# Moving the FFN units of a fused attention and mixture-of-depths kernel between scores and values, and the row fetch into a step of its own

## The chip, the cores and the metric

The kernel runs on one core of one Trainium2 chip. The metric is the device time of one execution in microseconds (us), the median of several runs. The core has a matrix engine (TensorE, PE in the profile, with its weight loads as PEld), a vector engine (VectorE, DVE), a scalar engine for activations and copies (ScalarE, ACT), a general engine (GpSimd, POOL) and a queue that issues most of the transfers (SyncE, SP).

## The reference

Attention with queries that are averaged in pairs is followed by a mixture of depths: in each batch the 128 tokens with the highest gate score go through a two-layer FFN, and the others pass unchanged.

```python
# q, k, v: (8, 8, 1152, 64) float32 = B, H, S, D
q_pool = q.reshape(B, H, S // 2, 2, D).mean(axis=3)
scores = scale * np.matmul(q_pool, k.transpose(0, 1, 3, 2))   # 576 x 1152 per head
attn = softmax(scores)                                        # over the 1152 keys
x = np.matmul(attn, v)            # then (B, S, H*D): 8 x 576 tokens x 512

scores = np.einsum('bsd,d->bs', x, w_gate)
out = x.copy()
for b in range(B):
    top_idx = np.argpartition(-scores[b], 128)[:128]
    xe = x[b, top_idx]
    ye = np.maximum(xe @ w1, 0.0) @ w2         # w1: 512 x 1024, w2: 1024 x 512
    g = 1.0 / (1.0 + np.exp(-scores[b, top_idx]))
    out[b, top_idx] = x[b, top_idx] + g[:, None] * ye
```

## The kernel before

Two heads of one batch are a pair; there are 32 pairs. The 576 pooled queries of a pair are worked in two halves of 288, so there are 64 halves, 8 to a batch. One turn `h` of the main loop issues the scores of half `h` and the values of half `h - 1`. The order in which instructions are issued here is the order in which each engine's queue gets them; nothing reorders them.

```python
for h in range(n_halves + 1):
    if h < n_halves:
        ...                                  # loads two pairs ahead; store of x
        self.scores(half)                    # PE L818, ACT exponentials L825
        if h > 1:
            of = halves[h - 2 - s]["pair"]
            if s == 0:                       # even half
                of["groups"] = self.side_by_side(of["sum"]...)   # ACT L887
            else:                            # odd half
                self.spread(of)              # ACT L902: total -> sums
        if h > 2:
            self.gated(halves[h - 3])        # DVE red, part; starts a batch's routing
        self.folded(half)                    # POOL acc L857, DVE fold L862, sum L872
        if h > 1:
            self.multiplied(halves[h - 2])   # POOL prod L925
        if s == 0 and loaded:
            upcoming = loaded
            self.prepare_pair(upcoming)      # POOL qp, DVE kT, qT of the next pair
    ...
    if h > 0:
        done = halves[h - 1]
        self.weighted(done)                  # PE L836, ACT two L844, POOL av L846
        self.drained(done)                   # DVE avb
    ...
    if 1 < h < n_halves and s == 0:
        done["pair"]["total"] = self.added(done["pair"]["groups"])   # DVE L893
    ...
    elif h > 2 and s == 1:
        self.normalized(halves[h - 2]["pair"])    # DVE rec, POOL x
    if h < n_halves:
        self.units()                         # one step of every batch's routing
```

The scores of a half are nine tiles of 128 keys, each in one PSUM tile of two banks. There are four such tiles, used in turn for everything that TensorE writes (`self.psum = pool("psum", 4, space=psum)`). An exponential on ScalarE takes each score tile to `p`, of which there are two buffers. The row sums of `p` come from `folded`: GpSimd adds the first two thirds of `p` into `acc`, and VectorE sums the last third and then `acc`.

The routing of a batch is a Python generator; each `yield` ends a step, and a call of `units()` runs one step of every batch in flight, the newest batch first. It starts in `gated` when a batch's last pair is done. Cut to what the engines do, for every batch but the last:

```python
def routed(self, b, part):
    nc.vector.tensor_reduce(line, part ...)           # the batch's gate scores
    yield True
    if b < self.B - 2:
        groups = self.side_by_side(line)              # ACT L887, 4 copies
        yield True
        total = self.added(groups)                    # DVE
    else:
        ...                                           # batch 6: one matmul, one copy
    ... sync DMAs: total -> row in DRAM -> sc_row, sc # scores on all partitions
    yield True
    if b < self.B - 2:
        yield True
    nc.gpsimd.tensor_scalar(gate ...)                 # POOL
    for t, rows in tiles:                             # rank of each token: comparisons
        ... 3 DVE operations per tile of tokens
        if t in (1, 3):
            yield True
    nc.scalar.activation(gate, gate, AF.Exp, scale=-1.0) ...
    ... sync DMAs: both -> row_rank in DRAM -> lines  # ranks and gates, all partitions
    yield True
    for of, to in ((self.token_line, found), (lines[:, :, 1, :], own_gate)):
        nc.vector.scalar_tensor_tensor(pick, lines, self.token, of ...)  # search, DVE
    nc.gpsimd.tensor_scalar(index, found ...)         # POOL
    nc.gpsimd.indirect_dma_start(xe <- rows_out[index])   # fetch of the rows
    yield True
    yield True
    ... 4 transposes of xe on PE (L1192); nc.scalar.copy(xeT)
    yield True
    ... first layer: 2 x 16 matmuls (L1203); ACT hT = relu, twice (L1211)
    yield "hidden" ...
    ... second layer: 8 matmuls (L1216)
    nc.scalar.activation(y, ps, AF.Copy, scale=own_gate)  # ACT L1235
    nc.gpsimd.tensor_tensor(xe = y + xe)              # POOL L1238
    nc.gpsimd.indirect_dma_start(rows_out[index] <- xe)   # rows written back
    yield True
```

The matmul steps inside the layers yield `False`, which does not end a step. Batch 5 stops after its first layer (`"hidden"`) and its second layer is kept for the end of the kernel, where batches 6 and 7 finish. Scores are written to the output by `stored` before the rows are fetched from there.

Of the kernel before, what the change touches and what calls it, by code (L numbers as in the profile page):

```python
# [21 lines left out]
def _rows_of(ap_1d: bass.AP, parts: int) -> bass.AP:  # L22

    return dataclasses.replace(ap_1d, ap=[[0, parts]] + [list(x) for x in ap_1d.ap])
# [3 lines left out]
def _any_scores(  # L28
# [446 lines left out]
    def run(units):  # L475
        for _ in units:
            pass
# [50 lines left out]
    for _ in range(2):  # L528
        advance(None)
        one, two = None, one  # L530
    run(routing)
    run(routed(B - 1, x))


class _Plain:
# [461 lines left out]
    def routed(self, b, part):  # L997
# [12 lines left out]
        if b < self.B - 1:  # L1010

            yield True
            if b < self.B - 2:
                groups = self.side_by_side(line)
                yield True
                total = self.added(groups)
            else:
                total = self.small.tile([BLK, self.QB], F32, name="total")
                ps = self.banks()[:, 0, 0 : self.QB]
                nc.tensor.matmul(  # L1020
                    ps,
                    lhsT=self.merge.rearrange("p g j -> p (g j)"),
                    rhs=line[:, :],
                    start=True,
                    stop=True,
                )
                nc.scalar.copy(total[:, :], ps[0:BLK, :])
            sc_row = ffn.tile([P, NT * P], F32, name="sc_row")
            row = self.dram.tile([Sp], F32, name="row")
            nc.gpsimd.memset(sc[:, NF:], 0.0)  # L1030
            nc.sync.dma_start(row.rearrange("(i n) -> i n", i=BLK), total[:, :])
            nc.sync.dma_start(sc_row[:, 0:Sp], _rows_of(row[:], P))
            nc.sync.dma_start(sc[:, 0:NF], row[0 : NF * P].rearrange("(t p) -> p t", p=P))
            nc.sync.dma_start(
                sc[0 : self.TAIL, NF:], row[NF * P :].rearrange("(t p) -> p t", p=self.TAIL)
# [6 lines that stand above are left out]
            diag = ffn.tile([P, self.QB, BLK], F32, name="diag", bufs=1)  # L1042
            nc.vector.tensor_tensor(
                out=diag[:, :, :],
                in0=line[:, :].unsqueeze(2).broadcast_to([P, self.QB, BLK]),
                in1=self.same[:, :].unsqueeze(1).broadcast_to([P, self.QB, BLK]),
                op=ALU.mult,
            )
            yield True
            sc_row = self.line_of_scores()  # L1050
            ps = self.banks()
            for s in range(2):
                nc.tensor.matmul(  # L1053
                    ps[:, s, 0 : self.HALF],
                    lhsT=self.ones[:, :],
                    rhs=diag[:, s * self.HB : (s + 1) * self.HB, :].rearrange("p n i -> p (n i)"),
                    start=True,
                    stop=True,
                )
            nc.scalar.copy(  # L1060
                sc_row[:, 0:Sp].rearrange("p (i s n) -> p s n i", s=2, n=self.HB),
                ps[:, :, 0 : self.HALF].rearrange("p s (n i) -> p s n i", i=BLK),
            )
            yield True
            self.columns(sc, sc_row)
# [66 lines left out]
        for s0, w in self.slots:  # L1132
# [3 lines left out]
            if b == self.B - 1:  # L1136

                nc.vector.tensor_tensor(
                    out=pick[:, :, 0:w],
                    in0=self.slot_f[:, s0 : s0 + w].unsqueeze(1).broadcast_to([P, NT, w]),  # L1140
                    in1=rank[:, :].unsqueeze(2).broadcast_to([P, NT, w]),
                    op=ALU.is_equal,
                )
                yield True
                ps = self.banks()[:, 0, 0:2]
                for t, rows in tiles:
                    nc.tensor.matmul(  # L1147
                        ps[0:w, :],
                        lhsT=pick[0:rows, t, 0:w],
                        rhs=meta[0:rows, t, :],  # L1150
                        start=(t == 0),
                        stop=(t == NT - 1),
                    )
                nc.scalar.copy(index[0:w, :], ps[0:w, 0:1])
                nc.scalar.copy(own_gate[0:w, :], ps[0:w, 1:2])
            else:
                yield True

                found = self.small.tile([P, 1], F32, name="found_token")
                for of, to in ((self.token_line, found), (lines[:, :, 1, :], own_gate)):  # L1160
                    nc.vector.scalar_tensor_tensor(
                        out=pick.rearrange("p t i -> p (t i)").rearrange("p (i t) -> p i t", t=NT)[0:w],
                        in0=lines[0:w, :, 0, :],
                        scalar=self.token[0:w, s0 // P : s0 // P + 1],
                        in1=of[0:w, :, :],
                        op0=ALU.is_equal,
                        op1=ALU.mult,
                        accum_out=to[0:w, :],
                    )
                nc.gpsimd.tensor_scalar(  # L1170
                    out=index[0:w, :],
                    in0=found[0:w, :],
                    scalar1=float(b * Sp),
                    scalar2=None,
                    op0=ALU.add,
                )
# [106 lines left out]
        )  # L1283
        return count_i

    def units(self):

        for entry in self.routing[::-1]:
            b, unit = entry
            if b in self.waiting:  # L1290
                continue
            end = next((mark for mark in unit if mark), None)
            if end is None:
                self.routing.remove(entry)
            elif end == "hidden" and b == self.B - 3:
                self.waiting.add(b)

    def run(self):
# [14 lines left out]
        for h in range(n_halves + 1):  # L1313
            if h < n_halves:
                n, s = divmod(h, 2)
                if s == 0:
                    pair = upcoming
                    if pair["hp"] == 0:
                        part = self.ffn.tile([P, self.NPAIR, self.QB], F32, name="part")
                    pair["part"] = part  # L1320
                else:
                    loaded = None
                    if n + 2 < len(pairs):
                        loaded = self.load_pair(*pairs[n + 2])
                        self.load_values(loaded)
                    if n > 1:
                        self.stored(halves[h - 4]["pair"])
                if h > 1:
                    next(weights, None)
                half = {"pair": pair, "s": s}  # L1330
                halves.append(half)
                self.scores(half)
                if h > 1:

                    of = halves[h - 2 - s]["pair"]
                    if s == 0:
                        of["groups"] = self.side_by_side(of["sum"].rearrange("p j n -> p (j n)"))
                    else:
                        self.spread(of)
                if h > 2:  # L1340
                    self.gated(halves[h - 3])
                self.folded(half)
                if h > 1:
                    self.multiplied(halves[h - 2])
                if s == 0 and loaded:
                    upcoming = loaded
                    self.prepare_pair(upcoming)
            else:
                self.stored(halves[h - 3]["pair"])
                self.gated(halves[h - 3])  # L1350
                self.multiplied(halves[h - 2])
                self.units()
            if h > 0:
                done = halves[h - 1]
                self.weighted(done)
                self.drained(done)
            if h == n_halves:
                self.multiplied(done)
                self.gated(halves[h - 2])
            if 1 < h < n_halves and s == 0:  # L1360
                done["pair"]["total"] = self.added(done["pair"]["groups"])
            if h == n_halves:
                self.normalized(done["pair"])
            elif h > 2 and s == 1:
                self.normalized(halves[h - 2]["pair"])
            if h < n_halves:
                self.units()
        for _ in weights:
            pass

# [90 lines left out]
```

## Time and profile before

| what | value |
|---|---|
| time, median of 3 runs | 708.12 us (708.08 to 708.34) |
| span of the profiled execution | 706.3 us |
| mean granted TensorE clock | 0.999 |
| transfers | 82.86 MB, mean 117 GB/s |
| scores matmuls L818 | 4608 records, 296.0 us busy |
| values matmuls L836 | 4608 records, 294.1 us busy |
| first FFN layer L1203 | 512 records, 59.3 us busy |
| second FFN layer L1216 | 128 records, 57.3 us busy |
| exponentials L825 | 576, mean 691 ns, 319.2 us busy |
| acc L857 on GpSimd | 192, mean 1413 ns, 266.1 us busy |

How to read it: a float32 matmul leaves two records, so 36 matmuls of a half are 72 records in a chain or a timeline. Busy times of matmuls count the time between start and end of pipelined instructions, so waiting that is shorter than the pipeline is not seen as idle. Line numbers are those of the kernel before; in the changed kernel the lines after the first edit lie one to six further on. In a timeline the columns are the start in us, the length in us, the engine, the line, the operation, output and input with their shapes, the count, and in brackets the idle time of the engine ahead of it with what ended that. In the chain of waits the columns are start, length, engine and what.

### The profile page before, as it was taken

To read this page: it belongs to the slowest core of one execution; us is meant where nothing else is said; L and a number is where in the kernel's file an instruction comes from. 1 tells how busy PE (TensorE), PEld (TensorE's weight loads), DVE (VectorE), ACT (ScalarE), POOL (GpSimd) and SP (SyncE) were. 2 spreads that over 40 slices of the span, in tenths; PEclk is the share of its full clock that TensorE was granted. 3 is DMA by queue.
4 is the path that set the end of the run, shared out by engine and by line. 5 is a ranking of instruction groups with operands and counts; after the bars stand their busy time and mean duration, and the time that the engine had idled before them with its cause. 6 is when DMAs were issued, how large, how long until landed. Compare 5 with 4: busy or idle time off the path is not lost.

```text
span 706.3 us, 23391 instructions
## 1 busy us (share of the span) xinstructions
PE 695.8 (99%) x9948; PEld 499.9 (71%) x9948; DVE 494.4 (70%) x793; ACT 442.8 (63%) x963; POOL 484.9 (69%) x452
## 2 busy tenths in 40 slices
PE   8999999999999999999999999999999999999996
PEld 5668889977857678577775777767776677767573
DVE  3877777896549965499654987549784597869540
ACT  6677777777547774477745777467754777577210
POOL 5877777877668685586955879557884777866520
PEclk9999999999999999999999999999999999999999
DMA  9888887849692296825867258652877428442200
GB/s 181 172 170 181 182 166 139 151 95 164 116 169 57 66 165 126 154 52 106 166 104 135 52 126 159 119 106 52 163 127 134 86 53 172 72 82 60 47 31 35
DMA packets 389490, 82.86 MB, mean 117 GB/s; under 512 B 376640, under 2 KB 376640, under 8 KB 389376
## 3 DMA queue, kind: packets, MB, share of 16 engines
q1 hardware_dynamic: 387872, 76.49, 57.4%
q0 software_dynamic: 1280, 4.20, 1.7%
q8 instruction: 80, 1.31, 0.8%
q10 hardware_dynamic: 224, 0.59, 0.3%
q14 instruction: 34, 0.28, 0.1%
HBM read 69.65 MB, written 11.59 MB: 115 GB/s over the span
## 4 chain that ended last, share of the span: by engine, by line
PE 92%; POOL 3%; issue 1%; DVE 1%; DMA 1%; ACT 1%; SPq 0%; POOLq 0%; DVEq 0%; ACTq 0%
PE ps L818 38%; PE ps L836 37%; PE ps L1203 8%; PE ps L1216 7%; POOL acc L857 2%; DMA kb<-in_k_dram 1%; PE ps L1192 1%; POOL prod L925 0%; ACT p L825 0%; POOL x L956 0%; DVE fold L862 0%; POOL av L846 0%; SPq L759 0%; PE ps L1147 0%; PE ps L1053 0%
## 5 line engine op out<-in xcount | busy, mean ns | idle before, releaser
L825 ACT ACTIVATE p<-ps 128x576 f32<-128x576 f32 x576 | 319.2, 691 | 2.6 <-PE ps L818 2.3
L857 POOL TENSOR_TENSOR acc<-p 128x576 f32<-128x576 f32 x192 | 266.1, 1413 | 50.4 <-ACT p L825 50.0
L818 PE MATMUL ps<-qT,kT 64*64 64x288 f32 x4608 | 296.0, 405 | 0.3 <-ACT p L825 0.3
L836 PE MATMUL ps<-p,v_sb 64*64 64x288 f32 x4608 | 294.1, 403 | 0.0
L836 PEld LDWEIGHTS ps<-p,v_sb 64*64 64x64 f32 x4608 | 213.2, 133 | 67.8 <-ACT p L825 14.3
L818 PEld LDWEIGHTS ps<-qT,kT 64*64 64x64 f32 x4608 | 193.3, 132 | 89.8 <-ACT p L825 18.5
L862 DVE TRANSPOSE_TENSOR_REDUCE fold<-p 128x54 f32<-128x1728 f32 x64 | 126.0, 1969 | 117.2 <-ACT p L825 117.2
L862 DVE TRANSPOSE_TENSOR_REDUCE fold<-acc 128x54 f32<-128x1728 f32 x64 | 124.8, 1951 | 42.0 <-POOL acc L857 41.9
L844 ACT COPY two<-ps 128x576 f32<-128x576 f32 x64 | 40.9, 638 | 126.1 <-PE ps L836 113.2
L846 POOL TENSOR_TENSOR av<-two 128x288 f32<-128x288 f32 x64 | 51.1, 798 | 28.9 <-ACT two L844 27.3
L956 POOL TENSOR_TENSOR x<-avb,rec 128x576 f32<-128x576 f32 x32 | 37.0, 1157 | 43.1 <-DVE rec L954 27.1
L1203 PEld LDWEIGHTS ps<-xeT,w 128*128 128x128 f32 x512 | 57.8, 192 | 2.7 <-issue 2.6
L1203 PE MATMUL ps<-xeT,w 128*128 128x128 f32 x512 | 59.3, 277 | 0.0
L1216 PE MATMUL ps<-w,hT 128*128 128x512 f32 x128 | 57.3, 598 | 0.0
L925 POOL TENSOR_TENSOR prod<-avb,w_gate 128x288 f32<-128x288 f32 x64 | 51.3, 802 | 0.6 <-DVE avb L915 0.6
L902 ACT ACTIVATE sums<-total,tiny 32x18 f32<-32x18 f32 x124 | 38.2, 308 | 13.1 <-DVE total L893 11.4
L732 POOL TENSOR_TENSOR qp<-qb 128x576 f32<-128x576 f32 x31 | 43.8, 1412 | 2.5 <-DMA qb<-in_q_dram 2.5
L1216 PEld LDWEIGHTS ps<-w,hT 128*128 128x128 f32 x128 | 23.6, 190 | 28.1 <-issue 28.0
L735 DVE STREAM_TRANSPOSE kT<-kb 128x1152 f32<-128x1152 f32 x31 | 42.5, 1369 | 0.0
L1211 ACT ACTIVATE hT<-ps 128x512 f32<-128x512 f32 x16 | 9.6, 597 | 47.7 <-PE ps L1203 47.7
L1238 POOL TENSOR_TENSOR xe<-y,xe 128x512 f32<-128x512 f32 x7 | 8.9, 1270 | 38.3 <-ACT y L1235 38.3
L915 DVE STREAM_TRANSPOSE avb<-av 128x288 f32<-128x288 f32 x64 | 29.2, 456 | 7.2 <-POOL av L846 7.2
(95 smaller groups left out, 326.1 us busy)
## 6 DMA issues: line engine op xcount, KB each, us to landing
kb<-in_k_dram SPq DMA_DIRECT2D x124, 144.0 KB, 3.6
qb<-in_q_dram SPq DMA_DIRECT2D x124, 144.0 KB, 3.9
v_sb<-in_v_dram SPq DMA_DIRECT2D x124, 144.0 KB, 3.4
out_dram<-x SPq DMA_DIRECT2D x128, 72.0 KB, 3.0
lines<-row_rank SPq DMA_DIRECT2D x7, 640.0 KB, 4.1
w<-in_moe_w_dram SPq DMA_DIRECT2D x8, 512.0 KB, 4.8
sc_row<-row SPq DMA_DIRECT2D x7, 288.0 KB, 3.4
acc<-in_q_dram ACTq DMA_DIRECT2D x2, 288.0 KB, 4.2
```

The costliest lines, as they stand in the source:

```text
L732: nc.gpsimd.tensor_tensor(out=qp[:, :, :], in0=pair["q"][:, :, 0, :], in1=pair["q"][:, :, 1, :], op=ALU.add)
L735: nc.vector.transpose(kT.rearrange("p (c g i) -> p c g i", c=self.NC, i=BLK), pair["k"].rearrange("p (g c) d -> p c g d", c=self.NC),)
L818: nc.tensor.matmul(sc[keys, j, 0:n], lhsT=pair["kT"][rows, c * P + keys.start : c * P + keys.stop], rhs=pair["qT"][rows, qs], start=True, ...
L825: nc.scalar.activation(p[:, c // G, c % G, :, :], sc[:, :, 0:n], AF.Exp, scale=self.scale)
L836: nc.tensor.matmul(av[j * self.D : (j + 1) * self.D, e, 0:n], lhsT=half["pair"]["v"][keys, j, c, :], rhs=half["p"][keys, c // G, c % G, j, :],
L844: nc.scalar.copy(two[:, :, :], av[:, :, 0:n])
L846: nc.gpsimd.tensor_tensor(out=half["av"][:, :], in0=two[:, 0, :], in1=two[:, 1, :], op=ALU.add)
L857: nc.gpsimd.tensor_tensor(out=acc[:, u, :], in0=units[:, 0, u, :], in1=units[:, 1, u, :], op=ALU.add)
L862: nc.vector.tensor_reduce(fold[:, a, :], of.rearrange("p u (m d) -> p (u m) d", d=BLK), AX.X, ALU.add, apply_transpose=True,)
L925: self.nc.gpsimd.tensor_tensor(out=pair["prod"][:, ns, :], in0=pair["avb"][:, ns, :], in1=self.w_gate[:, hp : hp + 1, :].broadcast_to([P, ...
L1203: nc.tensor.matmul(pv[:, f, 0:w], lhsT=self.w1[:, c, (f0 + f) * P : (f0 + f + 1) * P], rhs=xeT[:, c, 0:w], start=(c == 0), stop=(c == self ...
L1216: nc.tensor.matmul(ps[0:w, 0 : self.Dm], lhsT=hT[:, f, 0:w], rhs=self.w2[:, f, :], start=(f == 0), stop=(f == self.NFC - 1),)
```

## The change

It does two things. In the main loop, the routing steps of batches 0 to 5 are issued between the scores and the fold of a half, ahead of the values, where they stood behind the values; those of batch 6 (`b == self.B - 2`) stay behind the values. In the routing, an empty step is put ahead of the copies of `groups`, and another between the search for the tokens on VectorE and the index and fetch on GpSimd, both for batches 0 to 5 alone. It is meant to give ScalarE, which copies and scales what the units leave in PSUM, this work at a time when TensorE has the values to do and the next scores do not wait for it, and to keep GpSimd from standing while VectorE searches.

```diff
@@ routed
             yield True
             if b < self.B - 2:
+                yield True
                 groups = self.side_by_side(line)
                 yield True
                 total = self.added(groups)
@@ routed, behind the search
                         op1=ALU.mult,
                         accum_out=to[0:w, :],
                     )
+                if b < self.B - 2:
+                    yield True
                 nc.gpsimd.tensor_scalar(
                     out=index[0:w, :],
@@ units
-    def units(self):
+    def units(self, late):
         for entry in self.routing[::-1]:
             b, unit = entry
-            if b in self.waiting:
+            if b in self.waiting or late != (b == self.B - 2):
                 continue
@@ run
                 if h > 2:
                     self.gated(halves[h - 3])
+
+                self.units(late=False)
                 self.folded(half)
...
                 self.multiplied(halves[h - 2])
-                self.units()
+                self.units(late=True)
...
             if h < n_halves:
-                self.units()
+                self.units(late=True)
```

## The prediction

> **What bounds the kernel now.** I read the page's busy table first, then the chain of waits in order of time, then the timelines of ScalarE and GpSimd at the seams that the chain shows. The table:
>
> ```profile
> PE 695.8 (99%) x9948; PEld 499.9 (71%) x9948; DVE 494.4 (70%) x793; ACT 442.8 (63%) x963; POOL 484.9 (69%) x452
> ```
>
> TensorE is never idle, so the questions are how much of its time is waiting that counts as busy, and how near the other engines are to joining it. The chain, one batch of it (start, length, what):
>
> ```profile
> 257.83 0.59 PE ps L1192 x4
> 258.42 4.93 PE ps L818 x72
> 263.35 4.51 PE ps L836 x72
> 267.86 7.34 PE ps L1203 x64
> 275.20 4.53 PE ps L818 x72
> 279.73 4.37 PE ps L836 x72
> 284.09 7.06 PE ps L1216 x16
> 291.15 4.53 PE ps L818 x72
> 295.68 4.38 PE ps L836 x72
> 300.06 4.37 PE ps L818 x72
> ```
>
> L818 is a half's scores, L836 values, L1192 the transposes of the fetched rows, L1203 and L1216 the two FFN layers. Undisturbed scores or values take 4.37 us. The exceptions are what a better order could win: 0.56 on the scores after the transposes, 0.14 on the values behind them, 0.16 on scores after an FFN layer. ScalarE's timeline (start, length) shows why the first is so long:
>
> ```profile
> 257.92 0.64 ACT L844 COPY two<-ps 128x576 f32<-128x576 f32 x1 [1.27 <-PE ps L836]
> 258.58 0.85 ACT L887 COPY groups<-line 32x18 f32<-32x18 f32 x4
> 259.34 0.57 ACT L1195 COPY xeT<-ps 128x512 f32<-128x512 f32 x1
> 259.82 4.90 ACT L825 ACTIVATE p<-ps 128x576 f32<-128x576 f32 x9
> ...
> 291.19 0.69 ACT L1235 ACTIVATE y<-ps,own_gate 128x512 f32<-128x512 f32 x1 [6.34 <-PE ps L1216]
> ```
>
> The exponentials start 1.5 us after their scores (258.34 to 259.82), elsewhere 0.83 (299.87 to 300.70). A score tile needs one of four PSUM tiles, freed by an exponential, and those come every 0.54 us against 0.485 us a tile on TensorE. There is hardly any reserve: exponentials that start d late cost about d minus 0.1. GpSimd around the second FFN layer and around a row fetch, and two rows of the waits (total, times, longest):
>
> ```profile
> 291.96 1.27 POOL L1238 TENSOR_TENSOR xe<-y,xe 128x512 f32<-128x512 f32 x1 [6.24 <-ACT y L1235]
> 293.52 1.04 POOL L1239 DMA_INDIRECT out_dram<-xe,index  x1 [0.29 <-POOL xe L1238]
> 294.58 4.14 POOL L857 TENSOR_TENSOR acc<-p 128x576 f32<-128x576 f32 x3
> ...
> 332.78 0.92 POOL L1170 TENSOR_SCALAR index<-found_token 128x1 int32<-128x1 f32 x1 [2.97 <-DVE pick L1161]
> 333.97 1.13 POOL L1178 DMA_INDIRECT xe<-out_dram,index  x1 [0.28 <-POOL index L1170]
> ```
>
> ```profile
> POOL xe L1238 <- ACT y L1235: 38.3, 7, 6.8
> ACT sums L902 <- DVE total L893: 11.4, 6, 2.0
> ```
>
> GpSimd stands 6.2 us for the second layer, now harmlessly: its acc of the preceding half is long done, and the next acc has no input before about 295.1.
>
> **What the Trainium skill says.** "PSUM — Partial Sum Buffer", section "Engine vs sequencer instructions": the queues of ScalarE, VectorE and GpSimd are strict FIFO. The trace agrees: nothing of GpSimd's slips into those 6.24 us. "Perfetto Trace Analysis", section "Identifying the Most-Contended Engine": matmul busy share does not tell how near to the roofline TensorE is. It agrees too: the 4.93 us scores count as fully busy.
>
> **The change, part by part.** No instruction is added or removed; the number on each engine is equal. Two things move.
>
> (1) Units of batches 0 to 5 are issued after a half's exponentials and before its fold (acc on GpSimd, fold on VectorE). With L for the half in which a batch's line of scores is summed, and counting the two new empty steps, groups go from L to L+1, the comparisons from L+3..L+5 to L+4..L+6, search from L+6 to L+7, fetch from L+6 to L+8, transposes from L+8 to L+10, the layers from L+9 and L+10 to L+11 and L+12. The next batch's L is this one's L+8.
>
> *Gain.* ScalarE has about 2.9 us between its last exponential (1.5 us after the scores end) and the values' end (4.37 us). The 0.85 us of groups and 0.57 us of xeT now go there. Five places like 258 (0.56 + 0.14) and the first groups at 101, where the chain has 5.03 us from the end of the values to that of the scores against 4.37, and 4.51 for the values: 5 x 0.70 + 0.80 = 4.3 us. The 0.16 after an FFN layer I take to be the change between array shapes: it moves to the values, and the transposes now also have values behind them: 6 x 0.15 = 0.9 back.
>
> *Loss.* The wait for y now stands ahead of that half's own acc. I walk the four queues forward with durations from the timelines, zero at the start of the second layer (its half is L+4 of the next batch). GpSimd: layer 7.06, y done at 8.05, xe and scatter to 10.8, three accs to 14.9 (normally 3.8), prod 0.8, qp 1.4, to 17.1. VectorE: fold of acc to 17.0, sum 0.3, kT 1.3, qT 0.7 to 19.3, avb 0.4, total 0.3 to 19.9. TensorE: values to 11.6, next scores to 15.9, values to 20.3, scores again, which need qT at 20.3: just met. But ScalarE has the copies into sums (L902) after the exponentials of 17.5; they need the total, so run 20.0 to 21.2, and the copy of the values behind them ends at 21.8 instead of 21.25: **0.5 us** lost.
>
> The delay does not run out. Round the loop acc, fold, sum, kT, qT, avb, total, red, comparisons, fold p, fold acc, sum, avb, rec, x, back to acc, the pieces in microseconds are 4.15, 1.95, 0.3, 1.3, 0.7, 0.4, 0.3, 0.4, 2.8, 1.9, 1.95, 0.3, 0.4, 0.15, 1.15: 18.2 against 17.5 for two halves. So two halves on (L+6) acc is done at 33.3, the total at 38.3, sums to 39.6, the copy 0.9 late: **0.8 us** lost.
>
> (2) Fetch in a step of its own. Index and fetch are 2.3 us (332.78 to 335.13), now in half L+8 ahead of its acc, while GpSimd's x is late too: search (1.8) stands ahead of VectorE's fold. The acc ends at 52.8, about 5.4 late, the total at 57.4. In the next half ScalarE does sums (1.27) and then the next batch's groups (0.82) before the copy of the values: that ends at 60.2 instead of 57.6, and qT comes about 0.3 after the scores could start: **2.8 us** lost on the scores ahead of the transposes. The first layer's 7.34 us in the half after that lets everything catch up.
>
> *Sum.* 0.5 + 0.8 behind five second layers: 6.5. The 2.8 for batches 1 to 4: 11.2. Batch 0 has no second layer ahead of it: 2.5 by the same walk. Batch 5 is followed by batch 6, which has no groups on ScalarE: 1.5. Together 21.7, less 4.3, plus 0.9: 18.3. At the end TensorE waits 0.62 us for the last but one batch's rows (654.1 to 654.7); the first layer of batch 5 now stands two halves nearer to it, so the queues should be less late there: minus 0.6. 708.1 + 17.7 = 725.8; I say 725.5. The walk on the kernel before gives 86.0 us a batch, where the trace has 344.38 - 258.42 = 85.96; that is why I trust it.
>
> **Rivals.** *The gain alone.* ScalarE's blocked seams go, GpSimd and VectorE at 70% absorb the rest: 708.1 - 4.3 + 0.9, about 704.5. For it: GpSimd loses its 20.2 us of waiting for the search (7 waits of up to 3.0), and VectorE's comparisons fill its longest waits (117.2 us for exponentials). Against it: idle on these engines is spread over the span, and the place that matters is the one where GpSimd is made to stand. *Nothing.* qT is needed 1 us after it comes and the copies into sums could come late without harm if the slack is a little larger than I reckon: losses of 3 to 5 us against the gain, 706 to 710. *More of a wait.* If the rows of lines come after the search is issued (they have about 2 us to spare by my walk), or comparisons run at their longer times (some tie operations take 1.5 instead of 0.6 us), every lag grows, and as the loop already takes longer than two halves it falls on TensorE: 728 to 733. *TensorE's rhythm.* FFN matmuls between scores and values might lose more than 0.15 at each change of shape; at 0.5 that is 6 us more.
>
> **Range and chances.** Shifting single durations in the walk by the scatter that the timelines show (accs by 0.02, comparisons by a tenth, search by 0.2, fetch by 0.3) moves the difference between 16.5 and 19.6, but a wait which I have overlooked, or one that does not exist, is a matter of 5 to 8 us. So 716 to 731. The 2% line is at 722.3: slower 0.70, within 2% 0.27, faster 0.03.
>
> **What the profile after would show.** Right: transposes and both layers stand between L818 and L836 in the chain; the scores just before the transposes take about 7 us instead of 4.37 in batches 1 to 4, and the scores two and four halves behind the second layer about 0.5 and 0.8 too long; the wait of ScalarE's sums for VectorE's total grows from 11.4 us to some 45; GpSimd's wait for the search disappears, its wait for y stays near 38. Wrong: if scores before the transposes are at 4.4, the delay of acc is absorbed and the loop has more slack than I count; if loss stands at the values (L836) instead, it is the change of shape or the PSUM tiles; if sums hardly wait but the scores start late, it is qT.

## The result and the profile after

The changed kernel takes 731.29 us (median, 731.03 to 732.77) against 708.12 us: a ratio of 1.0329, 95% interval 1.0315 to 1.0342, or 23.2 us slower. That is 0.3 us above the predicted range. The profiled execution of it took 732.77 us: its clock was granted at 0.81 to 0.84 for the microseconds from 5 to 15, and its first values start at 19.29 us, where another execution of the same kernel, at full clock there, has 18.12 us. The later kernels ran in sets of their own, each beside fresh runs of the kernel before, whose medians were 708.15 to 710.77 us; so ratios are compared, and where one is turned into microseconds it is by 708.1.

The busy table of the page after:

```profile
PE 704.0 (96%) x9948; PEld 481.7 (66%) x9948; DVE 506.8 (69%) x793; ACT 445.6 (61%) x963; POOL 487.0 (67%) x452
```

TensorE's busy time has grown by 8 us and VectorE's by 12, though no instruction was added, and TensorE is now seen to be idle. TensorE's timeline of one batch, from its second layer (L1219) to the next batch's transposes (L1195):

```profile
304.65 7.13 PE L1219 MATMUL ps<-w,hT 128*128 128x512 f32 x16
...
324.86 4.99 PE L818 MATMUL ps<-qT,kT 64*64 64x288 f32 x72
329.67 4.60 PE L836 MATMUL ps<-p,v_sb 64*64 64x288 f32 x72
...
342.94 1.69 PE L818 MATMUL ps<-qT,kT 64*64 64x288 f32 x24
345.44 3.44 PE L818 MATMUL ps<-qT,kT 64*64 64x288 f32 x48 [0.82 <-ACT two L844]
348.71 4.60 PE L836 MATMUL ps<-p,v_sb 64*64 64x288 f32 x72
...
357.49 4.59 PE L836 MATMUL ps<-p,v_sb 64*64 64x288 f32 x72
362.99 1.69 PE L818 MATMUL ps<-qT,kT 64*64 64x288 f32 x24 [0.91 <-DVE qT L739]
366.24 3.38 PE L818 MATMUL ps<-qT,kT 64*64 64x288 f32 x48 [1.56 <-ACT two L844]
369.55 0.66 PE L1195 MATMUL ps<-ident,xe 128*128 128x128 f32 x4
```

Read from start to start, against 4.37 us: the scores at 324.86 lose 0.44 us, those at 342.94 lose 1.40. At 357.49 the next scores come 1.13 too late, and these scores lose another 2.19. Scores and values elsewhere lose 0.15 at most, up to a wait of 0.5 us at the end. Over all batches these places add up to 27.8 us. The brackets name the two ways in: qT late from VectorE, and the copy of the values (two) late from ScalarE, which holds the exponentials up. The waits (total, times, longest):

```profile
DVE fold L862 <- POOL acc L857: 90.1, 24, 11.2
ACT sums L902 <- DVE total L893: 58.0, 17, 4.6
POOL xe L1241 <- ACT y L1238: 49.0, 7, 8.4
PE ps L818 <- ACT two L844: 12.8, 11, 1.6
PE ps L818 <- DVE qT L739: 4.6, 6, 0.9
```

The first three were 41.9, 11.4 and 38.3 before. Put in order they are the chain: GpSimd waits for y, the fold for acc, sums for the total, and at last the scores for the copy (two) or for qT. The lines of GpSimd, VectorE and ScalarE around the second layer and the search, from the timeline:

```profile
312.59 1.27 POOL L1241 TENSOR_TENSOR xe<-y,xe 128x512 f32<-128x512 f32 x1 [8.38 <-ACT y L1238]
315.26 4.14 POOL L857 TENSOR_TENSOR acc<-p 128x576 f32<-128x576 f32 x3
319.44 1.98 DVE L862 TRANSPOSE_TENSOR_REDUCE fold<-acc 128x54 f32<-128x1728 f32 x1 [11.22 <-POOL acc L857]
...
341.30 4.72 POOL L857 TENSOR_TENSOR acc<-p 128x576 f32<-128x576 f32 x3
343.46 1.27 ACT L902 ACTIVATE sums<-total,tiny 32x18 f32<-32x18 f32 x4 [3.53 <-DVE total L893]
343.71 1.05 DVE L1162 SCALAR_TENSOR_TENSOR pick<-lines,token,token_line 128x640 f32<-128x640 f32 x1
344.81 1.90 DVE L1162 SCALAR_TENSOR_TENSOR pick<-lines,token 128x640 f32<-128x640 f32 x1
345.98 1.38 POOL L925 TENSOR_TENSOR prod<-avb,w_gate 128x288 f32<-128x288 f32 x1
```

The first three lines are as foretold: VectorE stands 11 us for an acc that GpSimd could not begin. The last five hold what was not foretold: the search takes 1.05 and 1.90 us. Before, VectorE's timeline had it so:

```profile
331.82 0.86 DVE L1161 SCALAR_TENSOR_TENSOR pick<-lines,token,token_line 128x640 f32<-128x640 f32 x1
332.72 0.89 DVE L1161 SCALAR_TENSOR_TENSOR pick<-lines,token 128x640 f32<-128x640 f32 x1
```

Beside the long search GpSimd's acc takes 4.72 us for 4.14, and prod 1.38 for 0.80.

### The profile page after: what moved, and what is told of

It is laid out like the page before. It is cut to its first block, busy times and chain, and to the rows that moved or that the text cites. A ratio compares the mean times of both kernels' runs of the same rounds, so it can differ in the third digit from the quotient of the medians.

```text
span 731.0 us, 23385 instructions
## 1 busy us (share of the span) xinstructions
PE 704.0 (96%) x9948; PEld 481.7 (66%) x9948; DVE 506.8 (69%) x793; ACT 445.6 (61%) x963; POOL 487.0 (67%) x452
## 4 chain that ended last, share of the span: by engine, by line
PE 57%; POOL 12%; DVE 10%; issue 9%; DMA 5%; ACT 4%; SPq 2%; POOLq 0%; DVEq 0%; ACTq 0%
PE ps L818 22%; PE ps L836 22%; POOL acc L857 7%; PE ps L1206 6%; PE ps L1219 6%; DVE fold L862 4%; DVE kT L735 2%; DMA out_dram<-x 2%; DMA kb<-in_k_dram 1%; ACT sums L902 1%; POOL prod L925 1%; ACT two L844 1%; DVE tie L1102 1%; ACT p L825 1%; DVE qT L739 1%
## 5 line engine op out<-in xcount | busy, mean ns | idle before, releaser
L818 PE MATMUL ps<-qT,kT 64*64 64x288 f32 x4608 | 301.6, 408 | 17.4 <-ACT two L844 12.8
L857 POOL TENSOR_TENSOR acc<-p 128x576 f32<-128x576 f32 x192 | 269.1, 1430 | 18.2 <-ACT p L825 17.8
L818 PEld LDWEIGHTS ps<-qT,kT 64*64 64x64 f32 x4608 | 184.9, 133 | 122.6 <-ACT p L825 33.5
L836 PEld LDWEIGHTS ps<-p,v_sb 64*64 64x64 f32 x4608 | 203.4, 133 | 78.2 <-ACT p L825 12.1
L1219 PE MATMUL ps<-w,hT 128*128 128x512 f32 x128 | 57.3, 598 | 0.0
L925 POOL TENSOR_TENSOR prod<-avb,w_gate 128x288 f32<-128x288 f32 x64 | 54.9, 858 | 0.6 <-DVE avb L915 0.6
L1219 PEld LDWEIGHTS ps<-w,hT 128*128 128x128 f32 x128 | 23.6, 190 | 28.1 <-issue 25.8
L887 ACT COPY groups<-sum 32x36 f32<-32x36 f32 x124 | 27.1, 219 | 9.7 <-DVE sum L872 8.3
```

The lines of the kernel that those rows point to most:

```text
L818: nc.tensor.matmul(sc[keys, j, 0:n], lhsT=pair["kT"][rows, c * P + keys.start : c * P + keys.stop], rhs=pair["qT"][rows, qs], start=True, ...
L836: nc.tensor.matmul(av[j * self.D : (j + 1) * self.D, e, 0:n], lhsT=half["pair"]["v"][keys, j, c, :], rhs=half["p"][keys, c // G, c % G, j, :],
L857: nc.gpsimd.tensor_tensor(out=acc[:, u, :], in0=units[:, 0, u, :], in1=units[:, 1, u, :], op=ALU.add)
L925: self.nc.gpsimd.tensor_tensor(out=pair["prod"][:, ns, :], in0=pair["avb"][:, ns, :], in1=self.w_gate[:, hp : hp + 1, :].broadcast_to([P, ...
L1219: nc.tensor.matmul(ps[0:w, 0 : self.Dm], lhsT=hT[:, f, 0:w], rhs=self.w2[:, f, :], start=(f == 0), stop=(f == self.NFC - 1),)
```

## The experiments

Two theories were to be told apart. **Queue**: GpSimd's work of a step ahead of acc makes acc late, and VectorE's and ScalarE's queues carry that to TensorE. **Contention**: VectorE's operations on two arrays, search and tie (the comparison of equal scores within the ranks), run long when GpSimd works beside them, which they do because GpSimd no longer stands for the search.

| kernel | ratio to before | 95% interval |
|---|---|---|
| changed kernel | 1.0329 | 1.0315 to 1.0342 |
| changed kernel again | 1.0332 | 1.0311 to 1.0354 |
| steps early, fetch with the search | 1.0454 | 1.0433 to 1.0474 |
| fetch step alone, steps late | 0.9985 | 0.9975 to 0.9996 |
| y added late | 1.0159 | 1.0140 to 1.0178 |
| fetch late | 1.0154 | 1.0136 to 1.0171 |
| both late | 1.0009 | 0.9999 to 1.0019 |
| one-array search | 1.0201 | 1.0183 to 1.0218 |
| one-array search and tie | 1.0119 | 1.0101 to 1.0136 |
| both late, one-array search | 0.9945 | 0.9925 to 0.9966 |
| only groups and transposes early | 0.9962 and 0.9960 | 0.9946 to 0.9975 |
| y late, search and fetch together late | 1.0043 | 1.0027 to 1.0059 |

### The two parts apart

The early steps without the separate fetch, from the changed kernel:

```diff
-                if b < self.B - 2:
-                    yield True
                 nc.gpsimd.tensor_scalar(
                     out=index[0:w, :],
```

> The steps of batches 0 to 5 stand between scores and values as in the changed kernel, but the fetch stays in the step of the search, so GpSimd stands for the search again. Queue theory (GpSimd's and VectorE's work of a step, put ahead of that half's acc, delays acc, and the delay runs through fold, total and sums into the next exponentials): most or all of the loss remains, about 734 us, since GpSimd now stands for the search ahead of an acc too. Theory that the separate fetch is the culprit: it falls back to 705 to 710 us. Theory of contention between the search and acc: the two search operations return to 0.86 and 0.89 us from 1.02 and 1.76.

Measured: 1.0454, or 32 us, more than the 26 expected. Placing the steps early is the whole loss, and the separate fetch takes part of it back. The search is at 0.86 and 0.89 us (medians): GpSimd stands for it again.

The separate fetch in the kernel before, all steps behind the values (the same two lines, added):

> The kernel before with the fetch alone in a step of its own, all steps behind the values. Queue theory: the fetch is one turn later but stays where it has always stood, 708 to 710 us. If the separate fetch were the culprit: over 720 us. Contention theory: GpSimd no longer stands while VectorE searches, so the search operations grow from 0.86 and 0.89 us towards 1.0 and 1.8 us, and the acc beside them from 1.4 to over 1.5 us, though the total hardly moves; if the search stays at 0.9 us, contention with GpSimd is not what made it longer.

Measured: 0.9985; the fetch step by itself is even a hair faster. But its timeline shows the long search by itself, with every step still behind the values:

```profile
331.97 4.73 POOL L857 TENSOR_TENSOR acc<-p 128x576 f32<-128x576 f32 x3
334.03 1.40 DVE L1161 SCALAR_TENSOR_TENSOR pick<-lines,token,token_line 128x640 f32<-128x640 f32 x1
335.48 1.91 DVE L1161 SCALAR_TENSOR_TENSOR pick<-lines,token 128x640 f32<-128x640 f32 x1
336.67 1.38 POOL L925 TENSOR_TENSOR prod<-avb,w_gate 128x288 f32<-128x288 f32 x1
```

The search takes 1.40 and 1.91 us where the kernel before has 0.86 and 0.89, and GpSimd again has 4.73 and 1.38 us for acc and prod. The total does not suffer, so VectorE had the room for it here.

### GpSimd's part of the steps behind the values

From the changed kernel; a step can now ask to go on behind the values of its turn:

```diff
+                if b < self.B - 3:
+                    yield "late"
                 nc.gpsimd.tensor_tensor(out=xe[0:w, :], in0=y[0:w, :], in1=xe[0:w, :], op=ALU.add)
@@ units
-            if b in self.waiting or late != (b == self.B - 2):
+            if b in self.waiting or late != self.late.get(b, b == self.B - 2):
                 continue
             end = next((mark for mark in unit if mark), None)
+            if b < self.B - 2:
+                self.late[b] = end == "late"
```

> The changed kernel, but the addition of y and the write back (GpSimd) are issued behind the values of the turn; y itself (ScalarE) and the fetch stay. Queue theory: the wait of GpSimd for y no longer delays acc; the 0.45 and 1.4 us of loss two and four halves behind the second layer go and part of the 3.3 us ahead of the transposes, about 9 us in all: 721 to 723 us. If the wait for y is harmless: 731 us.

Measured: 1.0159, which is 719.4 us on the scale of 708.1, or 12 us given back where 9 were expected. The fetch alone:

```diff
                 if b < self.B - 2:
                     yield True
+                    yield "late"
                 nc.gpsimd.tensor_scalar(
                     out=index[0:w, :],
```

> The changed kernel, but index and fetch are issued behind the values of the turn in which they stand; the wait for y stays ahead of acc. Queue theory: the loss ahead of the transposes (3.3 us a batch) goes for the most part, the 0.45 and 1.4 us stay: 719 to 722 us. If index and fetch (1.4 us of GpSimd) are too short to matter: 729 to 731 us.

Measured: 1.0154, or 719.0 us. Its timeline has 0.45 and 1.41 us left behind the second layer, as the queue theory has it, and ahead of the transposes still 1.5 of the 3.3 us. Both edits together:

> The changed kernel, but everything of a step that GpSimd would do ahead of acc (addition of y and write back; index and fetch) is issued behind the values of that turn; matmuls, ScalarE's and VectorE's parts of the steps stay between scores and values. Queue theory: acc is on time, about 21 us come back: 705 us if the search stays short, 710 if it is still long. Theory that the change of array shape or the PSUM tiles cost the time: no change from 731 us.

Measured: 1.0009: 22.7 of 23.3 us come back, with all matmuls still between scores and values. So the change of array shape (64x64 for scores and values, 128x128 for the layers and the transposes) and the PSUM tiles are not the cause. What is left stands in its timeline, ahead of the transposes:

```profile
352.55 1.27 ACT L902 ACTIVATE sums<-total,tiny 32x18 f32<-32x18 f32 x4 [2.69 <-DVE total L893]
353.84 0.85 ACT L887 COPY groups<-line 32x18 f32<-32x18 f32 x4
354.60 0.62 ACT L844 COPY two<-ps 128x576 f32<-128x576 f32 x1
355.28 3.14 PE L818 MATMUL ps<-qT,kT 64*64 64x288 f32 x44 [0.85 <-ACT two L844]
```

This is the same way in, with only the long search (1.05 and 1.91 us here too) to drive it.

### The contention by itself

The changed kernel, with the search on one array. It counts instead of finding the token; fixed rows (tokens 1 to 128) are fetched, so the addresses of the row transfers change too:

```diff
-                    nc.vector.scalar_tensor_tensor(
+                    nc.vector.tensor_scalar(
                         out=pick...,
                         in0=lines[0:w, :, 0, :],
-                        scalar=self.token[...],
-                        in1=of[0:w, :, :],
+                        scalar1=self.token[...], scalar2=None,
                         op0=ALU.is_equal,
-                        op1=ALU.mult,
+                        op1=ALU.add,
                         accum_out=to[0:w, :],
                     )
...
-                    scalar1=float(b * Sp), scalar2=None, op0=ALU.add,
+                    scalar1=self.token[0:w, 0:1], scalar2=float(b * Sp),
+                    op0=ALU.add, op1=ALU.add,
```

> The changed kernel, but the two search operations read one array (ranks) instead of two and count instead of finding the token; the fetched rows are then fixed ones of the batch (tokens 1 to 128) and the gate is 1, so the output differs. All queues and counts are the same. Contention theory (two-array operations of VectorE run long beside GpSimd): search back to 0.8 to 0.9 us each, total about 726 to 727 us, which is the missed part of the prediction. If the search is long for another reason, it stays at 1.0 and 1.8 us and the total at 731 us.

Measured: 1.0201, 9.1 us less than the changed kernel, twice what was expected. The searches take 0.87 us each (median), no acc is over 1.46 us, where one of the changed kernel takes 1.99. That is an operation of the length that the two-array search has undisturbed (0.86 and 0.89), so what was taken away is the standing of VectorE beside GpSimd.

The one-array search is also another operation (tensor_scalar for scalar_tensor_tensor), so this kernel alone does not tell the second array from the operation. `part`, a tensor_tensor of two small arrays (red and rec) that every kernel has, helps. In the changed kernel it runs beside x on GpSimd and ends with it:

```profile
332.84 1.16 POOL L956 TENSOR_TENSOR x<-avb,rec 128x576 f32<-128x576 f32 x1 [4.89 <-DVE rec L954]
333.11 0.92 DVE L981 TENSOR_TENSOR part<-red,rec 128x18 f32<-128x18 f32 x1
```

In the kernel before there is one place where GpSimd does nothing beside it:

```profile
618.35 0.18 DVE L981 TENSOR_TENSOR part<-red,rec 128x18 f32<-128x18 f32 x1
```

So two different operations with two arrays run long beside GpSimd, while a comparison with one array (cmp, 128x448) takes 0.67 us beside acc in the kernel before and 0.68 us in the changed kernel where GpSimd stands. Then tie as well, for batches 0 to 6, without the mask of earlier tokens:

```diff
-                nc.vector.scalar_tensor_tensor(out=tie..., in0=sc_row..., scalar=own,
-                    in1=self.before..., op0=ALU.is_equal, op1=ALU.mult, accum_out=parts...)
+                nc.vector.tensor_scalar(out=tie..., in0=sc_row..., scalar1=own,
+                    scalar2=None, op0=ALU.is_equal, op1=ALU.add, accum_out=parts...)
```

> As the one-array search in the changed kernel, and for batches 0 to 6 the tie operation of the comparisons (two arrays) also reads one array; it leaves out the mask of earlier tokens, so ranks are one too high and the output differs. Contention theory: tie stays near 0.35 us where it took 0.97 and 1.02 us, and the scores four halves behind the second layer lose about 0.8 us, as the walk said, instead of 1.4: about 3 us less than with the one-array search alone (ratio 1.020), a ratio of 1.015 to 1.016. If the 1.4 us come from another wait, the ratio stays at 1.020.

Measured: 1.0119, 5.8 us less again, for 3 expected. Its group of tie operations, and its scores four halves behind the second layer with the values after them:

```profile
L1113 DVE TENSOR_SCALAR_CACHE_REDUCE tie<-sc_row,gate_sc x35: 263/329/343, 131.8 to 651.2; 128x128 f32<-128x128 f32 x28, 64x64 f32<-64x64 f32 x7
```

```profile
337.98 4.96 PE L818 MATMUL ps<-qT,kT 64*64 64x288 f32 x72
342.77 4.59 PE L836 MATMUL ps<-p,v_sb 64*64 64x288 f32 x72
```

tie takes 0.33 us (middle of the three, in ns), and these scores lose 342.77 - 337.98 - 4.37 = 0.42 us in place of 1.40. In batches 1 to 5 of the changed kernel tie takes 0.35 us where GpSimd stands for y, and 0.76 to 1.02 us beside GpSimd's work.

Both mends together, GpSimd's work late and the one-array search:

> The changed kernel with both mends: GpSimd's part of the steps behind the values, and the one-array search (fixed rows, output differs). If the two causes are the whole loss, only the gain is left: 0.4 to 0.6% under the kernel before. If more than 1% above the kernel before is left, there is a third cause.

Measured: 0.9945. No third cause is needed. This kernel also shows when a long operation costs nothing. Its tie still reads two arrays, and one in each of batches 1 to 5 takes 4.97 to 4.99 us, past three accs of GpSimd:

```profile
225.04 4.99 DVE L1102 SCALAR_TENSOR_TENSOR tie<-sc_row,gate_sc,before 128x128 f32<-128x128 f32 x1
225.75 4.13 POOL L857 TENSOR_TENSOR acc<-p 128x576 f32<-128x576 f32 x3
```

With acc on time VectorE has the room even for this. On the same chip the changed kernel again:

> The changed kernel unaltered, on the same chip as the two others, as their measure: 3.3% above the kernel before by every theory; anything else means that chips differ.

Measured: 1.0332.

### A version faster than both

From the kernel before, with only the two steps early for which ScalarE had been late (each turn now runs the steps marked early ahead of the fold and the others behind the values; those lines are not shown):

```diff
             yield True
             if b < self.B - 2:
+                yield "early"
                 groups = self.side_by_side(line)
-                yield True
+                yield "late"
@@ behind the fetch
             yield True
-            yield True
+            yield "early" if b < self.B - 2 else True
             xeT = ffn.tile(...)                   # transposes
             ...
-            yield True
+            yield "late" if b < self.B - 2 else True
```

> The kernel before, with only the two steps that ScalarE was late for put between scores and values: the copies of groups, and the transposes with the copy of xeT. Layers, comparisons, search (with the wait of GpSimd) and fetch stay behind the values. Queue theory: the gain of the change without its loss, 708.1 - 4.3 + 0.9 = 704.7 us. If the gain never existed (the long scores after the transposes come from the transposes themselves): 708 us.

> The kernel before with only the copies of groups and the transposes between scores and values, again, beside the other: 0.38% under the kernel before as measured; the order of the two is open.

Measured: 0.9962 (0.9948 to 0.9975) and 0.9960 (0.9946 to 0.9974), or 2.8 us, for 3.4 expected. TensorE around the transposes:

```profile
334.34 4.82 PE L818 MATMUL ps<-qT,kT 64*64 64x288 f32 x72
339.10 0.66 PE L1193 MATMUL ps<-ident,xe 128*128 128x128 f32 x4
339.68 4.60 PE L836 MATMUL ps<-p,v_sb 64*64 64x288 f32 x72
```

The scores that lost 0.56 us behind the transposes are gone from there; 0.2 to 0.4 us remain ahead of them (here 339.10 - 334.34 - 4.37 = 0.39). Last, the changed kernel with y added late, and search, index and fetch together behind the values:

```diff
+                if b < self.B - 3:
+                    yield "late"
                 nc.gpsimd.tensor_tensor(out=xe[0:w, :], in0=y[0:w, :], in1=xe[0:w, :], op=ALU.add)
@@ ahead of the search
                 yield True
+                if b < self.B - 2:
+                    yield "late"
                 found = self.small.tile(...)
@@ behind the search
-                if b < self.B - 2:
-                    yield True
```

> The changed kernel with GpSimd's addition of y behind the values, and search, index and fetch together behind the values, so that GpSimd stands while VectorE searches. Both causes of the loss are then away without leaving out any work. Queue and contention theory: search at 0.86 and 0.89 us, acc on time, and the gain is left: 0.4 to 0.6% under the kernel before. If only one of the two mends works, it is level with the kernel before.

Measured: 1.0043, a miss. The timeline tells why:

```profile
254.62 0.79 DVE L1164 SCALAR_TENSOR_TENSOR pick<-lines,token,token_line 128x640 f32<-128x640 f32 x1
254.78 1.64 POOL L956 TENSOR_TENSOR x<-avb,rec 128x576 f32<-128x576 f32 x1 [1.55 <-DVE rec L954]
255.45 1.66 DVE L1164 SCALAR_TENSOR_TENSOR pick<-lines,token 128x640 f32<-128x640 f32 x1
256.40 0.80 POOL L1173 TENSOR_SCALAR index<-found_token 128x1 int32<-128x1 f32 x1
```

In that place GpSimd does not stand: x is released by the rec just ahead of the search, so x and the search run side by side, and both are long (x 1.64 us for 1.16). That is not the whole miss. In batches 1 to 5 about 0.76 us is lost before the search begins, at the scores from 249.84 on, and ScalarE waits for a late total there too:

```profile
249.72 1.27 ACT L902 ACTIVATE sums<-total,tiny 32x18 f32<-32x18 f32 x4 [2.75 <-DVE total L893]
```

So acc was not on time: with the fetch one half earlier, the second layer falls on a half in which GpSimd has x to do as well, and the fold at 225.64 waits 2.59 us for the acc behind it. No run isolates this.

## Why the prediction was wrong in its size

*The mechanism held.* Second layer, y, acc, fold, total, sums, copy of the values, exponentials, scores: each link is in the waits above, and moving GpSimd's part away took 22.7 us back. *The gain held:* 4.3 less 0.9 was predicted, and the kernels that keep it without the loss are at 0.9945 and 0.9960, that is 3.9 and 2.8 us. *Change of shape:* values behind an FFN layer or transposes at 4.52 to 4.57 us, as put.

*The step that failed* is the durations in the walk round the loop. It took "comparisons 2.8" and "search (1.8)" from the kernel before and moved them to where GpSimd works. In the changed kernel two ties of the comparisons, and the accs two and four halves behind the late one (315.26, above), are

```profile
325.53 1.02 DVE L1102 SCALAR_TENSOR_TENSOR tie<-sc_row,gate_sc,before 128x128 f32<-128x128 f32 x1
327.35 0.76 DVE L1102 SCALAR_TENSOR_TENSOR tie<-sc_row,gate_sc,before 128x128 f32<-128x128 f32 x1
334.30 4.16 POOL L857 TENSOR_TENSOR acc<-p 128x576 f32<-128x576 f32 x3
354.37 4.14 POOL L857 TENSOR_TENSOR acc<-p 128x576 f32<-128x576 f32 x3
```

and the same ties in the kernel before

```profile
314.25 0.55 DVE L1101 SCALAR_TENSOR_TENSOR tie<-sc_row,gate_sc,before 128x128 f32<-128x128 f32 x1
315.60 0.63 DVE L1101 SCALAR_TENSOR_TENSOR tie<-sc_row,gate_sc,before 128x128 f32<-128x128 f32 x1
```

From the end of the late acc to that of the next in the list are 19.06 us, where the walk has 18.2. Of the difference 0.6 is the two ties (comparisons 3.37 us for 2.77), and 0.3 an operation of GpSimd on the gates just ahead of that acc, which the walk left out. From there to the end of the last acc are 20.05 us, where the walk has 19.5 (33.3 to 52.8): the search measured 1.05 + 1.90 = 2.95 us, 1.2 more than before, and index with fetch 1.7 for 2.3, since index took 0.23 us for 0.92.

The terms of the sum that follow: scores two halves behind the second layer 0.45 for 0.5, right; four halves behind it 1.4 for 0.8; ahead of the transposes, batches 1 to 4, 3.3 for 2.8; batch 0, 3.1 for 2.5; batch 5, 2.1 for 1.5. Together 27.8 for 21.7. The second term falls to 0.4 with tie on one array (0.33 us, less than tie takes in the kernel before), so the length of tie sets it. The third falls to about 2.1 with the one-array search, which is as short as the walk had it: there the walk was too high, index and fetch among the reasons, and this hid part of the 1.2 us that the long search adds. Its own sums also have two slips: 14.9 + 18.2 is 33.1 and not 33.3, and from an acc to the total its pieces add up to 4.95 us, where the last stretch has 4.6 (52.8 to 57.4); together they are worth some 0.15 us.

So of the 27.2 us between the gain alone (0.9945) and the changed kernel (1.0329), 9.1 go with the search's second array and 5.8 with tie's; the other 12.3 us are the displaced queue with both operations short, less than the walk's 21.7. The walk had part of the contention in it unseen, since comparisons taken from the kernel before already ran beside GpSimd there. These shares hold in this order only. Taken the other way round, GpSimd's part behind the values gives 22.7 us back and leaves 4.5 for the search: a long operation costs only where its queue is late already.

*The end:* the wait of 0.62 us for the rows of batch 6 should have gone; 0.30 us of it is still there. *Signs foretold:* the wait of sums went to 58.0 us for "some 45", and that for y grew to 49.0, not "near 38", because GpSimd reaches it earlier. One reading was off without effect: the acc behind the second layer had its input before 295.1, for it starts at 294.58 in the prediction's own lines. The rival "More of a wait" named longer ties and 728 to 733 us; of its two reasons this one came true, and the other did not, since the search never waited for the rows of `lines`. It did not name the longer search.

The warning was in the kernel before. Its index operation took 0.92 us for one element a row, and 0.23 us in the changed kernel; there it ran beside the second search operation, here after it. And `part` took 0.89 us there in the median, for the 0.18 of the undisturbed one. "GPSIMD Engine Reference", section "8. Key points", in the Trainium skill names the condition, VectorE instructions with two SBUF inputs, and the runs agree: search and tie are long with two arrays, not with one. "SBUF — State Buffer", section "🔬 SBUF: two separate sides", says that one then waits for the other's whole instruction. `part` fits: it ends 0.03 us after x. The long search fits roughly: it begins at 344.81 while the third acc runs, and ends at 346.71, 0.69 us after that acc (341.30 + 4.72 = 346.02); undisturbed it takes 0.89. The tie of 4.99 us does not: it stood for three accs and not for one. A run that isolates one pair of instructions was not made, so the order in which the two engines are let in stays open.

## What to carry to other kernels

Filling the time of a full engine moves work ahead of something on every other queue, so ask of each in-order queue what now waits behind it: here the addition of y with its write back ahead of acc cost 12 us, more than all that the move could bring. Move only the instructions of the engine that was late (the two ScalarE steps, 0.4% faster), and leave the rest. A wait that looks wasteful may keep two engines from running side by side; before taking it away, look for operations beside it that are short only because the other stands.

## What was not expected of the hardware

VectorE's scalar_tensor_tensor of 128 x 640 with both inputs in SBUF went from 0.89 to 1.91 us beside GpSimd's additions, and these from 1.41 to as much as 1.99 us and from 0.80 to 1.38: both sides lose. One-array operations of the same size stayed at 0.87 us beside the same additions. A tie of 128 x 128 took 0.35 us with GpSimd standing and up to 4.99 us where GpSimd went through three additions meanwhile.
